# Square root on ScalarE, a six-slot ring for residual tiles and stores one cycle late, in a transformer layer on one core

## The chip, the cores and the metric

The kernel runs on one core of one Trainium2 chip, as one program with one launch. The metric is device time in microseconds (us), the median of several executions of the same program. The kernel before takes 717.07 us (three executions, 716.6 to 718.04). A profile adds what each engine did; the time of an execution is some 2 us more than the span from its first to its last instruction (708.25 against 706.2 in one execution of the changed kernel).

## The reference

One transformer layer: attention over a sliding window of 256 with 32 heads of 32, and a two-matrix MLP with silu, both behind a layer norm and with a residual. Everything is bf16, S = 2048, D = 1024, F = 3584.

```python
def _layernorm(x, axis=-1, eps=1e-5):
    m = jnp.mean(x, axis=axis, keepdims=True)
    v = jnp.var(x, axis=axis, keepdims=True)
    return (x - m) / jnp.sqrt(v + eps)

def reference(A_x, A_wqkv, A_wo, B_x, B_w1, B_w2):
    def _A_ref(x, wqkv, wo):
        ...  # 32 heads, causal window of 256, softmax(q k^T / sqrt(32)) v
        return o.transpose(0, 2, 1, 3).reshape(B, S, D) @ wo
    def _B_ref(x, w1, w2):
        return silu(x @ w1) @ w2
    x = A_x
    h = x + _A_ref(_layernorm(x), A_wqkv, A_wo)
    h2 = h + _B_ref(_layernorm(h), B_w1, B_w2)
    return h2
```

## The kernel before

The sequence is cut into four blocks of 512 rows, each of four tiles of 128. The order of instructions is written by hand (a manual schedule); nearly every transfer is issued by SyncE (SP), in program order. SP also waits: a transfer that isn't ready holds up every transfer behind it. A plan of the program, with the part names used below:

1. First block: statistics, reciprocal root and normalisation of the four tiles of x, transposes on TensorE, and the V projection, tile by tile; then Q and K of block 0.
2. Three loops of 24 cycles: attention of block b-1 beside V, Q and K of block b.
3. The last attention loop: 24 cycles of attention of block 3 beside the output projection of blocks 0 to 2, and beside the second layer norm of block 0, in single steps.
4. MLP of block 0. Its first h1 groups carry the end of the attention of the last head group (g = 7), and its h1 groups 6 to 13 the output projection of block 3. Then the MLP of blocks 1 to 3.

The first block. The tile's reciprocal root is an integer guess and three Newton steps, twelve small operations on VectorE, and one PSUM tile takes all eight transposes:

```python
def ln_rstd(st, rs, lo, hi):
    ...
    nc.vector.tensor_scalar(out=va, in0=st[:, lo:hi, 1], scalar1=LN_EPS, scalar2=None, op0=ALU.add)
    ...  # shift, subtract from 0x5F3759DF
    for _ in range(3):
        nc.vector.scalar_tensor_tensor(out=ta, in0=y, scalar=-0.5, in1=va, op0=ALU.mult, op1=ALU.mult)
        nc.vector.tensor_tensor(out=ta, in0=ta, in1=y, op=ALU.mult)
        nc.vector.scalar_tensor_tensor(out=y, in0=ta, scalar=1.5, in1=y, op0=ALU.add, op1=ALU.mult)

for j in range(4):
    ln_stats(x_ring[j], st, j)
    ln_rstd(st, rs, j, j + 1)
    ln_norm(x_ring[j], st, rs, j)
    ln_transpose(x_ring[j], lnT_b[0], j, act)
    v_group(0, j, 0, act)
    v_group(0, j, 1, act)
```

An output-projection group: eight matmuls, one for each head group's transposed attention output, then the residual add and, after the second half, the store of h. Two slots for the residual tile, two for the result:

```python
def load_res(b, j, src):
    nc.sync.dma_start(out=t_in[j % 2], in_=src[(b * 4 + j) * P:(b * 4 + j + 1) * P, :])

def wo_group(b, j, c):
    acc = next_acc()
    for g in range(G):
        nc.tensor.matmul(acc, lhsT=qT[b][:, g, j * P:(j + 1) * P], rhs=wo[:, g, c * 512:(c + 1) * 512], ...)
    nc.vector.tensor_tensor(out=t_out[j % 2][:, c * 512:(c + 1) * 512], in0=acc,
                            in1=t_in[j % 2][:, c * 512:(c + 1) * 512], op=ALU.add)
    if c == 1:
        nc.sync.dma_start(out=h_dram[...], in_=t_out[j % 2])
```

The last attention loop, and the start of the MLP:

```python
for g in range(G):
    for kind in KINDS:
        scores(NB - 1, g, kind)
        b, j, c = dense[n]
        if c == 0:
            ...
            load_res(nb, nj, x2d)          # the next tile's residual
        wo_group(b, j, c)
        if pending:
            pending.pop(0)()               # attention output of head group g-1; its end issues
                                           # the transpose of that group into qT
        ...                                # w1 rows, one every second cycle
        if n == 9:
            steps = ln2_steps(0)
            steps.pop(0)()                 # load of h, 1 MB, into h_blk
        if n == 17:
            nc.sync.dma_start(out=w2[0], in_=w2_v[:, 0:4, :])
        for _ in range(2 if n % 3 == 0 else 1):
            if steps and n >= 14:
                steps.pop(0)()             # 4 x statistics, rstd, 4 x norm, 4 x transpose
        n += 1
    pending = tail_of(NB - 1, g)
...
load_res(NB - 1, 0, x2d)
load_w2(5)
for b in range(NB):
    extra = []
    if b == 0:
        extra = [(f, 1) for f in pending]  # three parts: the last attention outputs and their transpose
    for ft in range(FT):
        acc = h1_group(b, ft)
        if extra:
            extra.pop(0)[0]()
            if not extra and b == 0:
                for i in (1, 2, 3, 4):
                    load_w2(i)             # 1 MB each
        silu(b, acc, ft)
        if b == 0 and 6 <= ft < 14:
            ...
            wo_group(NB - 1, j, c)
```

The softmax here doesn't subtract the row's maximum and nothing guards it: scores larger than these inputs give would overflow.

## Time and profile before

| | before |
|---|---|
| time, median (lowest, highest) | 717.07 us (716.6, 718.04) |
| span of the profiled execution (its time) | 717.0 us (718.72) |
| TensorE busy | 691.0 us |
| mean granted TensorE clock | 0.992 |

First from the page: the busy time of each engine, with its share of the span and its number of instructions. Then the view of waits, for TensorE (PE): which group of instructions stood idle, for whom, how long in all, how often, and the longest.

```profile
PE 691.0 (96%) x4916; PEld 333.4 (47%) x5006; DVE 292.9 (41%) x645; ACT 257.1 (36%) x325; POOL 172.8 (24%) x375
```

```profile
engine line waited for: us in total, times, longest us
PE acc L417 <- DMA r_a<-r_a: 6.6, 1, 6.6
PE acc L198 <- ACT r_w L179: 4.5, 4, 1.1
PE acc L216 <- DVE r_t L218: 3.8, 3, 1.6
```

L417 are the h1 matmuls, released by a transpose of the second norm; L198 are the V matmuls of the first block, which wait for ScalarE's copies of the transposes; L216 are the output-projection groups, which wait for an accumulator that VectorE's residual add (L218) frees. Together they are 15 us. Most of what else the change could give back is TensorE's slow clock around those holes: in the first block sixteen V matmuls take 5.20 us at a granted clock of 0.52 (9.5 to 13.0 us), and 3.63 later.

### The profile page before, as it was taken

Reading aid. Unit: us, or ns where it says so; the run is one execution under the profiler, and the core shown is the slowest. Engines: PE = TensorE matmul, PEld = TensorE weight load, DVE = VectorE, ACT = ScalarE, POOL = GpSimd, SP = SyncE. Lnnn points to the kernel's source line nnn. Section 1 sums busy time; section 2 is a strip of 40 time slices with the busy share of each in tenths; the row PEclk is TensorE's granted clock in tenths of the full one; section 3 lists DMA queues with packets and bytes.
Section 4 is the critical chain, followed back from the end, with each engine's and each line's share of the span. In section 5 each row is a group of like instructions: output and inputs, shape, how many; then the busy total and the mean of one; then the engine's idle time right before and its main releaser. Section 6 shows DMA issues by size and latency. Waiting matters only on the chain.

```text
span 717.0 us, 12077 instructions
## 1 busy us (share of the span) xinstructions
PE 691.0 (96%) x4916; PEld 333.4 (47%) x5006; DVE 292.9 (41%) x645; ACT 257.1 (36%) x325; POOL 172.8 (24%) x375
## 2 busy tenths in 40 slices
PE   7899999999999999869999999999999999999998
PEld 2444555555555555434444444444444444444443
DVE  7265745844344345724341613425133352234111
ACT  2315667777777776611230003310033200133000
POOL 1004657777777676600000000000000000000000
PEclk9999999999999999989999999999999999999999
DMA  9440133122401589757104140021310032300110
GB/s 312 157 91 28 23 61 89 24 46 52 135 17 23 134 278 326 217 146 296 45 2 138 60 111 0 1 65 54 81 37 0 1 96 61 80 1 0 30 37 22
DMA packets 75112, 60.56 MB, mean 84 GB/s; under 512 B 48944, under 2 KB 59184, under 8 KB 75056
## 3 DMA queue, kind: packets, MB, share of 16 engines
q1 hardware_dynamic: 75056, 59.78, 29.4%
q8 instruction: 39, 0.64, 0.4%
q14 instruction: 17, 0.14, 0.1%
HBM read 39.85 MB, written 8.39 MB: 67 GB/s over the span
## 4 chain that ended last, share of the span: by engine, by line
PE 91%; DMA 3%; DVE 2%; SPq 1%; ACT 1%; issue 1%; POOL 1%; DVEq 0%; POOLq 0%; ACTq 0%
PE hacc L417 18%; PE hacc L455 17%; PE acc L206 16%; PE acc L455 10%; PE acc L417 9%; PE acc L198 8%; PE o_ps L270 4%; PE sc L234 4%; PE acc L216 3%; DMA r_t<-in_A_x_dram 3%; PE hacc L216 1%; SPq L175 1%; DVE r_t L218 1%; POOL r_e L260 1%; ACT r_w L179 1%
## 5 line engine op out<-in xcount | busy, mean ns | idle before, releaser
L260 POOL TENSOR_SCALAR_AFFINE_SELECT r_e<-r_e 128x256 bf16<-128x256 bf16 (+1 forms) x368 | 169.9, 490 | 130.9 <-ACT r_e L245 127.4
L245 ACT ACTIVATE r_e<-sc 128x1024 bf16<-128x1024 f32 (+2 forms) x192 | 175.8, 967 | 70.2 <-PE sc L234 57.3
L417 PEld LDWEIGHTS <-r_w 128*128 128x128 bf16 x896 | 87.7, 98 | 112.4 <-issue 8.3
L455 PEld LDWEIGHTS <-r_a 128*128 128x128 bf16 x896 | 87.7, 98 | 105.7
L455 PE MATMUL hacc<-r_a 128*128 128x512 bf16 x548 | 121.7, 379 | 0.6
L417 PE MATMUL hacc<-r_e,r_w 128*128 128x512 bf16 x444 | 100.2, 379 | 0.6
L426 ACT ACTIVATE r_n<-hacc 128x512 f32<-128x512 f32 x30 | 17.9, 597 | 178.9 <-PE hacc L417 178.9
L455 PE MATMUL acc<-r_a 128*128 128x512 bf16 x328 | 73.6, 379 | 0.4
L206 PEld LDWEIGHTS <-r_w 128*128 128x128 bf16 x512 | 46.2, 98 | 58.6 <-issue 8.9
L208 DVE CAST r_a<-acc 128x512 bf16<-128x512 f32 x56 | 38.6, 690 | 84.6 <-PE acc L206 59.4
L270 PEld LDWEIGHTS <-r_e 128*128 128x128 bf16 x1440 | 50.4, 96 | 23.0 <-issue 0.6
L206 PE MATMUL acc<-r_t,r_w 128*128 128x512 bf16 x240 | 60.0, 380 | 0.8
L206 PE MATMUL acc<-r_w 128*128 128x512 bf16 x246 | 57.7, 380 | 0.5
L216 PE MATMUL acc<-r_o,r_a 128*128 128x512 bf16 x196 | 48.7, 380 | 4.5 <-DVE r_t L218 3.8
L270 PE MATMUL o_ps<-r_a,r_e 128*128 128x33 bf16 x1440 | 51.2, 178 | 0.0
L417 PE MATMUL acc<-r_e,r_w 128*128 128x512 bf16 x216 | 49.1, 379 | 0.0
L216 PEld LDWEIGHTS <-r_a 128*128 128x128 bf16 x256 | 23.4, 98 | 33.4 <-issue 8.8
L234 PE MATMUL sc<-r_a 32*128 32x128 bf16 (+2 forms) x704 | 37.2, 276 | 0.1
L468 DVE SCALAR_TENSOR_TENSOR r_t<-hacc,r_t 128x512 bf16<-128x512 f32 x20 | 13.6, 682 | 56.6 <-PE hacc L455 56.6
L198 PE MATMUL acc<-r_w 128*128 128x512 bf16 x122 | 31.0, 395 | 4.9 <-ACT r_w L179 4.5
L468 DVE SCALAR_TENSOR_TENSOR r_t<-acc,r_t 128x512 bf16<-128x512 f32 x12 | 8.3, 691 | 64.2 <-PE acc L455 59.7
L427 DVE SCALAR_TENSOR_TENSOR r_a<-r_n,hacc 128x512 bf16<-128x512 f32 x30 | 20.6, 688 | 33.0 <-ACT r_n L426 33.0
(58 smaller groups left out, 429.6 us busy)
## 6 DMA issues: line engine op xcount, KB each, us to landing
r_w<-in_B_w_dram SPq DMA_DIRECT2D x8, 896.0 KB, 6.6
r_a<-in_B_w_dram SPq DMA_DIRECT2D x7, 1024.0 KB, 5.6
r_w<-in_A_wqkv_dram SPq DMA_DIRECT2D x6, 1024.0 KB, 11.4
r_o<-in_A_x_dram SPq DMA_DIRECT2D x16, 256.0 KB, 5.1
r_t<-in_A_x_dram SPq DMA_DIRECT2D x16, 256.0 KB, 4.9
h_dram<-r_t SPq DMA_DIRECT2D x16, 256.0 KB, 4.0
r_t<-h_dram SPq DMA_DIRECT2D x16, 256.0 KB, 2.8
out_dram<-r_t SPq DMA_DIRECT2D x32, 128.0 KB, 1.7
```

The costliest lines, as they stand in the source:

```text
L198: nc.tensor.matmul(acc, lhsT=lnT_b[b % 2][:, kt, j * P:(j + 1) * P], rhs=wqkv[:, kt, col0:col0 + 512], start=(kt == 0), stop=(kt == KT - 1))
L206: nc.tensor.matmul(acc, lhsT=wqkv[:, kt, col0:col0 + P], rhs=lnT_b[b % 2][:, kt, :], start=(kt == 0), stop=(kt == KT - 1))
L208: copy(out=(qT, kT)[which][b][:, g, :], in_=acc)
L216: nc.tensor.matmul(acc, lhsT=qT[b][:, g, j * P:(j + 1) * P], rhs=wo[:, g, c * 512:(c + 1) * 512], start=(g == 0), stop=(g == G - 1))
L234: nc.tensor.matmul(sc[hh // 2][:, hh % 2, ch * P:(ch + nq) * P], lhsT=kT[t // 4][r0:r0 + DH, g, (t % 4) * P:(t % 4 + 1) * P], rhs=qT[b][r0 ...
L245: nc.scalar.activation(out=e[:, :, lo:hi], in_=sc[pair][:, :, lo:hi], func=ACT.Exp, scale=scale)
L260: nc.gpsimd.affine_select(out=ap, in_=ap, pattern=[[0, 2], [0, n], [sgn, P]], compare_op=ALU.is_ge if upper else ALU.is_gt, fill=0.0, base ...
L270: nc.tensor.matmul(o_ps[pair][:, qt * 2 + hh, 0:VW], lhsT=e_of(i, kind, pair)[:, hh, ch * P:(ch + 1) * P], rhs=v[:, b * 4 + kt, g * 4 + pa ...
L417: nc.tensor.matmul(acc, lhsT=w1[:, kt, ft * P:(ft + 1) * P], rhs=ln2T[b][:, kt, :], start=(kt == 0), stop=(kt == KT - 1))
L427: nc.vector.scalar_tensor_tensor(out=gT[:, ft, :], in0=th, scalar=1.0, in1=acc, op0=ALU.add, op1=ALU.mult)
L455: nc.tensor.matmul(acc, lhsT=gT[:, ft, j * P:(j + 1) * P], rhs=w2[ft // 4][:, ft % 4, c * 512:(c + 1) * 512], start=(ft == 0), stop=(ft == ...
L468: nc.vector.scalar_tensor_tensor(out=t_out[j % 2][:, c * 512:(c + 1) * 512], in0=acc, scalar=0.5, in1=t_in[j % 2][:, c * 512:(c + 1) * 512 ...
```

## The change

The intent is to remove these three. In the first block the root goes to ScalarE, the norm and the transposes are done in two halves (with two PSUM tiles), and tile j+1 is made ready before the V groups of tile j. The residual tiles of x get a ring of six slots, four of which lie in space of Q and K that is dead by then, so that they are loaded far ahead. The stores of h and the transposes of attention outputs go on a list `late` that is emptied at the start of the next cycle, so that SP doesn't wait for them while other transfers could be issued. The second norm's steps start two cycles earlier.

```diff
-    tp_ps = o_ps[1][:].rearrange("p a b -> p (a b)").bitcast(BF16)
+    tp_ps = [t[:].rearrange("p a b -> p (a b)").bitcast(BF16) for t in o_ps]
+    r_in = [view(r_a, 16384, 1024), view(r_a, 17408, 1024), *t_in, view(r_a, 22528, 1024), view(r_a, 23552, 1024)]
     load_x(0, 0)
-    load_wqkv(2 * D)
+    load_wqkv(2 * D, 0, 4)
     load_x(0, 1)
+    load_wqkv(2 * D, 4, 8)
     load_wqkv(2 * D + 512)
 ...
+    def ln_first(xt, st, rs, j):
+        ln_stats(xt, st, j)
+        nc.scalar.activation(out=rs[:, j:j + 1], in_=st[:, j, 1:2], func=ACT.Sqrt, bias=eps[:], scale=1.0)
+        nc.vector.reciprocal(out=rs[:, j:j + 1], in_=rs[:, j:j + 1])
+        for h in range(2):
+            ln_norm(xt[:, h * 512:(h + 1) * 512], st, rs, j)
+
+    def turn_first(xt, dst, j):
+        for h in range(2):
+            ...  # four transposes into tp_ps[h], then a ScalarE copy of 512 columns
 ...
+    def load_res(t):
+        nc.sync.dma_start(out=r_in[t % 6], in_=x2d[t * P:(t + 1) * P, :])
+    late = []
+    def run_late():
+        while late:
+            late.pop(0)()
 ...
-            nc.sync.dma_start(out=h_dram[...], in_=t_out[j % 2])
+            late.append(lambda: nc.sync.dma_start(out=h_dram[...], in_=t_out[j % 2]))
 ...
             attn_out(b, g, 11, 16)
-            attn_transpose(b, g)
+            late.append(lambda: attn_transpose(b, g))
 ...
+    ln_first(x_ring[0], st, rs, 0)
+    turn_first(x_ring[0], lnT_b[0], 0)
     for j in range(4):
-        ln_stats(...); ln_rstd(...); ln_norm(...); ln_transpose(...)
+        if j < 3:
+            ln_first(x_ring[j + 1], st, rs, j + 1)
         v_group(0, j, 0, act)
+        if j < 3:
+            turn_first(x_ring[j + 1], lnT_b[0], j + 1)
         v_group(0, j, 1, act)
+        if j == 2:
+            nc.scalar.activation(out=dummy[:], in_=eps[:], func=ACT.Exp)     # table load, early
 ...
-        return steps                                             # second norm: all norms, then all transposes
+        return steps[:-2] + [turns[0], steps[-2], turns[1], steps[-1]] + turns[2:]
 ...
     for g in range(G):                                           # last attention loop
         for kind in KINDS:
+            run_late()
+            if n % 2 == 0 and n >= 2 and n // 2 + 5 < S // P:
+                load_res(n // 2 + 5)
 ...
-            for _ in range(2 if n % 3 == 0 else 1):
-                if steps and n >= 14:
+            for _ in range(1 if n < 17 else 2):
+                if steps and n >= 12:
                     steps.pop(0)()
 ...
+    run_late()
     load_w2(5)
     ...
         for ft in range(FT):
             acc = h1_group(b, ft)
+            run_late()
             if extra:
                 extra.pop(0)[0]()
                 if not extra and b == 0:
                     for i in (1, 2, 3, 4):
                         load_w2(i)                               # unchanged
```

More of the change, by code (lines that the diff above doesn't have):

```diff
@@ L125, in load_x, with load_wqkv @@
         nc.sync.dma_start(out=x_ring[(b % 2) * 4 + j], in_=x2d[(b * 4 + j) * P:(b * 4 + j + 1) * P, :])
-    def load_wqkv(c0):
-        nc.sync.dma_start(out=wqkv[:, :, c0:c0 + 512], in_=wqkv_v[:, :, c0:c0 + 512])
+    def load_wqkv(c0, k0=0, k1=KT):
+        nc.sync.dma_start(out=wqkv[:, k0:k1, c0:c0 + 512], in_=wqkv_v[:, k0:k1, c0:c0 + 512])
     load_x(0, 0)
-    load_wqkv(2 * D)
+    load_wqkv(2 * D, 0, 4)
     load_x(0, 1)
+    load_wqkv(2 * D, 4, 8)
     load_wqkv(2 * D + 512)
@@ L140 @@
     make_identity(nc, ident[:])
+    eps = const.tile([P, 1], F32, name="eps")
+    nc.vector.memset(eps[:], LN_EPS)
     warm = ebuf[0]
@@ L171, in ln_norm, with ln_transpose @@
                                 op0=ALU.subtract, op1=ALU.mult)
-    def ln_transpose(xt, dst, j, copy):
-        if copy is None:
-            nc.sync.dma_start_transpose(out=dst[:, :, j * P:(j + 1) * P], in_=xt)
-            return
-        for kt in range(KT):
-            nc.tensor.transpose(out=tp_ps[:, kt * P:(kt + 1) * P], in_=xt[:, kt * P:(kt + 1) * P], identity=ident[:])
-        copy(out=dst[:, :, j * P:(j + 1) * P], in_=tp_ps.rearrange("p (k q) -> p k q", q=P))
+    def ln_transpose(xt, dst, j):
+        nc.sync.dma_start_transpose(out=dst[:, :, j * P:(j + 1) * P], in_=xt)
+    def ln_first(xt, st, rs, j):
[6 more added lines that the diff above has]
+        for h in range(2):
+            for i in range(4):
+                kt = h * 4 + i
+                nc.tensor.transpose(out=tp_ps[h][:, i * P:(i + 1) * P], in_=xt[:, kt * P:(kt + 1) * P], identity=ident[:])
+            nc.scalar.copy(out=dst[:, h * 4:(h + 1) * 4, j * P:(j + 1) * P],
+                           in_=tp_ps[h][:, 0:512].rearrange("p (k q) -> p k q", q=P))
     def ln_tiles(tag):
@@ L208, in qk_group, with load_h @@
         copy(out=(qT, kT)[which][b][:, g, :], in_=acc)
-    def load_res(b, j, src):
-        nc.sync.dma_start(out=t_in[j % 2], in_=src[(b * 4 + j) * P:(b * 4 + j + 1) * P, :])
+    def load_h(b, j):
+        nc.sync.dma_start(out=t_in[j % 2], in_=h_dram[(b * 4 + j) * P:(b * 4 + j + 1) * P, :])
+    def load_res(t):
[4 more added lines that the diff above has]
+            late.pop(0)()
     def wo_group(b, j, c):
@@ L218, in wo_group @@
         nc.vector.tensor_tensor(out=t_out[j % 2][:, c * 512:(c + 1) * 512], in0=acc,
-                                in1=t_in[j % 2][:, c * 512:(c + 1) * 512], op=ALU.add)
+                                in1=r_in[(b * 4 + j) % 6][:, c * 512:(c + 1) * 512], op=ALU.add)
         if c == 1:
-            nc.sync.dma_start(out=h_dram[(b * 4 + j) * P:(b * 4 + j + 1) * P, :], in_=t_out[j % 2])
+            late.append(lambda: nc.sync.dma_start(out=h_dram[(b * 4 + j) * P:(b * 4 + j + 1) * P, :], in_=t_out[j % 2]))
     def e_of(i, kind, pair):
@@ L302 @@
     st, rs = ln_tiles("a")
+    ln_first(x_ring[0], st, rs, 0)
+    turn_first(x_ring[0], lnT_b[0], 0)
     for j in range(4):
-        ln_stats(x_ring[j], st, j)
-        ln_rstd(st, rs, j, j + 1)
-        ln_norm(x_ring[j], st, rs, j)
-        ln_transpose(x_ring[j], lnT_b[0], j, act)
+        if j < 3:
+            ln_first(x_ring[j + 1], st, rs, j + 1)
         v_group(0, j, 0, act)
+        if j < 3:
+            turn_first(x_ring[j + 1], lnT_b[0], j + 1)
         v_group(0, j, 1, act)
+        if j == 2:
+            dummy = small.tile([P, 1], F32, name="dummy", tag="dummy")
+            nc.scalar.activation(out=dummy[:], in_=eps[:], func=ACT.Exp)
     for j in range(4):
@@ L319, in ln1_steps @@
             steps.append(lambda j=j: ln_norm(xs[j], st, rs, j))
-        return steps, [lambda j=j: ln_transpose(xs[j], lnT_b[b % 2], j, None) for j in range(4)]
+        return steps, [lambda j=j: ln_transpose(xs[j], lnT_b[b % 2], j) for j in range(4)]
     def ln2_steps(b):
@@ L330, in ln2_steps @@
             steps.append(lambda j=j: ln_norm(hb[:, j, :], st, rs, j))
-        for j in range(4):
-            steps.append(lambda j=j: ln_transpose(hb[:, j, :], ln2T[b], j, None))
-        return steps
+        turns = [lambda j=j: ln_transpose(hb[:, j, :], ln2T[b], j) for j in range(4)]
+        return steps[:-2] + [turns[0], steps[-2], turns[1], steps[-1]] + turns[2:]
     steps = sum(ln1_steps(1), [])
@@ L355 @@
             nc.sync.dma_start(out=wo[:, 4:8, :], in_=wo_v[:, 4:8, :])
+            load_res(0)
+            load_res(1)
         n = 0
@@ L376 @@
                 dense.append((b, j, c))
-    load_res(0, 0, x2d)
+    for t in range(2, 6):
+        load_res(t)
     steps = []
@@ L381 @@
         for kind in KINDS:
+            run_late()
+            if n % 2 == 0 and n >= 2 and n // 2 + 5 < S // P:
+                load_res(n // 2 + 5)
             scores(NB - 1, g, kind)
-            b, j, c = dense[n]
-            if c == 0:
-                nb, nj = (b, j + 1) if j < 3 else (b + 1, 0)
-                if nb < NB - 1:
-                    load_res(nb, nj, x2d)
-            wo_group(b, j, c)
+            wo_group(*dense[n])
             if pending:
@@ L427, in silu @@
         nc.vector.scalar_tensor_tensor(out=gT[:, ft, :], in0=th, scalar=1.0, in1=acc, op0=ALU.add, op1=ALU.mult)
-    load_res(NB - 1, 0, x2d)
+    run_late()
     load_w2(5)
@@ L437 @@
             acc = h1_group(b, ft)
+            run_late()
             if extra:
@@ L445 @@
                 j, c = divmod(ft - 6, 2)
-                if c == 0 and j < 3:
-                    load_res(NB - 1, j + 1, x2d)
                 wo_group(NB - 1, j, c)
-        load_res(b, 0, h_dram)
+        load_h(b, 0)
         if b == 0:
@@ L459 @@
             if j < 3:
-                load_res(b, j + 1, h_dram)
+                load_h(b, j + 1)
             accs = [next_acc(), next_acc()]
```

## The prediction

> **What bounds the kernel now.** I read the page first. TensorE is busy for 691.0 of 717.0 us and is 91% of the chain that ended last, so only TensorE's holes and its slow clock can be saved: 26 us at most, plus what the clock loses. The slices show where.
>
> ```profile
> PE   7899999999999999869999999999999999999998
> PEclk9999999999999999989999999999999999999999
> ```
>
> There are two weak places: the first two slices of 17.9 us, and the 18th and 19th (305 to 340 us). The waits of the whole run agree: between 60 and 236 us and after 320 us none is put down to PE. Then I read the timeline of 0 to 60 us:
>
> ```profile
> start us, us, engine line op out<-in xcount [idle before <-releaser]
> 1.52 5.51 PE L147 MATMUL sc<-r_e 128*128 128x512 bf16 x14 [1.52 <-DVE r_e L142]
> ...
> 4.96 0.21 DVE L154 BATCH_NORM_AGGREGATE st_a<-ln_st 128x2 f32<-128x12 f32 x1
> ...
> 7.52 0.55 DVE L170 TENSOR_SCALAR r_o<-r_o,st_a,rs_a 128x1024 bf16<-128x1024 bf16 x1
> ...
> 8.12 0.62 PE L178 MATMUL o_ps<-ident,r_o 128*128 128x128 bf16 x8 [1.09 <-DVE r_o L170]
> ...
> 8.78 1.01 ACT L179 COPY r_w<-o_ps 128x1024 bf16<-128x1024 bf16 x1 [6.69 <-PE o_ps L178]
> ...
> 9.84 5.20 PE L198 MATMUL acc<-r_w 128*128 128x512 bf16 x16 [1.10 <-ACT r_w L179]
> ...
> 27.07 3.63 PE L198 MATMUL acc<-r_w 128*128 128x512 bf16 x15 [1.15 <-ACT r_w L179]
> ...
> 30.54 27.79 PE L206 MATMUL acc<-r_w 128*128 128x512 bf16 x126
> ```
>
> Statistics end at 5.17, Newton's steps for the reciprocal root take VectorE to 7.48. Every tile then repeats transposes, a copy with TensorE idle 1.1 us, and 16 V matmuls. V takes 5.20 us the first time, 3.63 the last. Q/K begin at 30.54.
>
> Last, TensorE's timeline and the DMA queue's timeline at the end of attention:
>
> ```profile
> 244.24 1.89 PE L216 MATMUL acc<-r_o,r_a 128*128 128x512 bf16 x7 [0.87 <-DVE r_t L218]
> ...
> 276.37 1.89 PE L216 MATMUL acc<-r_o,r_a 128*128 128x512 bf16 x7 [1.39 <-DVE r_t L218]
> ...
> 293.48 1.89 PE L216 MATMUL acc<-r_o,r_a 128*128 128x512 bf16 x7 [1.57 <-DVE r_t L218]
> ...
> 302.88 0.53 PE L270 MATMUL o_ps<-r_a,r_e 128*128 128x33 bf16 x15
> 309.97 0.58 PE L417 MATMUL acc<-r_a,r_w 128*128 128x512 bf16 x1 [6.56 <-DMA r_a<-r_a]
> 310.77 2.76 PE L417 MATMUL acc<-r_a,r_w 128*128 128x512 bf16 x6 [0.22 <-DMA r_t<-in_A_x_dram]
> 313.33 0.57 PE L270 MATMUL o_ps<-r_a,r_e 128*128 128x33 bf16 x15
> ```
>
> ```profile
> 318.98 1.19 SPq L290 DMA_TRANSPOSE r_a<-r_n  x1
> 320.21 2.59 SPq L408 DMA_DIRECT2D r_a<-in_B_w_dram  x4
> 322.85 0.54 SPq L211 DMA_DIRECT2D r_t<-in_A_x_dram  x1
> ```
>
> Three output-projection groups wait for the residual add, which itself waits for residual loads. Then the first h1 group waits 6.56 us for transposes of the second layer norm, issued until 306.75, and starts slow.
>
> **What the Trainium skill says.** "TensorE: Matmul & The Clock Gate", Part 1: without recent work the array runs at half clock; the state is decided in free-running windows of about 3.4 us. The trace agrees: the V weight loads from 9.84 come every 0.43 us, from 13.15 twice as fast; the warm-up's last ones, near 6.2, were fast already, and the hole up to 9.84 cost that. "ScalarE: Activation LUTs", What ACT_TABLE_LOAD costs: 1283 ns a load, and square root and exp lie in different sets. The trace has one load of 1.28 us; the changed program has two. "DMA: Bandwidth & Descriptors", Queues, rings and completion order: within one issuer's ring the descriptors are taken in order. The trace agrees: the transpose issued at 270.50, alone 2.4 us, took 8.7 us and landed at 279.2, after a w1 load of 268.42 (9.7 us, 278.1); the residual load of 322.85, behind four w2 loads of 1 MB, took 11.7 us. So what stands behind megabytes in the SP order pays for them.
>
> **Part 1, the first block.** Statistics end at 5.2; square root on ScalarE (estimate 0.3 with a pointer bias, from the same skill section), reciprocal 0.2 (the attention reciprocals take 0.20), half a normalisation 0.3 (half of 0.55): ready at 6.1. But the 14 warm-up matmuls hold TensorE to 7.03, and some 0.15 more, since a memset of eps now precedes theirs. So transposes begin at 7.2 rather than 8.12, and the half copy (0.59 for 512 columns, as the V copies) releases V at 8.25 rather than 9.84. V of tile 0, half 0, needs both halves of the first weight megabyte; it landed at 6.6 before, about 8.0 now because x tile 1 goes between. From there transposes stand one tile ahead, so copies are hidden. Warm, V half 0 ends near 10.0, but weights of half 1 land only at 11.3 (issued 2.34, 9.0 to landing): start 11.3. Cold, it ends at 11.7, with transposes 12.2. Seven V groups of 1.73 and two more tiles of transposes at 0.5 follow: 13.1. VectorE and ScalarE just keep up: after a V group copy 0.59, root 0.3, reciprocal 0.2, half norm 0.3, against 1.73. The exp table load hides behind V of tile 3. Q/K begin at 24.4 to 25.5, not 30.54: gain 5.0 to 6.1, taken as 5.6. Q/K weights landed at 15.8 and 18.7, no bound.
>
> **Part 2, residual ring.** Tiles are loaded up to five ahead, the first two before the loop. The three waits go: 0.87 + 1.39 + 1.57 = 3.8 us. The rest of the loop, 24 cycles of about 2.57 us, is TensorE work and stays.
>
> **Part 3, second layer norm.** Its steps start two cycles earlier and go twice per cycle from cycle 17; transposes are issued after cycles 18 to 20, not 21 to 23. From cycle 20 to the loop's end are 4 x 2.57 = 10 us; two transposes of 1.3 us issue and 3.3 to landing fit. The h1 group starts where the loop ends. Before, from 303.41 to the next attention matmuls at 313.33 passed 9.9 us for 1.73 of work: gain 8.2, of which 6.8 is waiting and 1.4 the slow clock.
>
> **Part 4, what the lateness costs.** The last head group's transpose is now issued one h1 group later than its attention ends, but the four w2 loads stay where they were: in the changed order five w2 loads stand ahead of it, in the old only one. Call T0 the start of h1. The first four loads wait for nothing after T0+2; the fifth waits for the last attention matmuls, T0+6.6. Landings: the first 5.1 us after issue (as at 309.89), T0+7.1; then 2.7 us each (320.2 to 322.0 landed at 325.8, 328.5, 331.2, 333.9): the fifth T0+17.9, and the transpose behind it T0+18.6. The first output-projection group of the last block needs it in its eighth matmul. Before, it began 11.2 us after the second h1 group (313.76 to 324.95); adding 2.2 for the first gives T0+13.35, and seven matmuls of 0.216 make T0+14.9. New wait 3.8 us, and most likely a cold clock after it, 1.5 us, as after the old hole: loss 5.3.
>
> Sum: 5.6 + 3.8 + 8.2 - 5.3 = 12.3; less 0.3 for small waits of VectorE in the loop: 717.07 - 12.0 = 705.0 us, 1.7% less.
>
> **Rivals.** A: the late transpose is not held up. For it: it is small. Against: the order on the queue and the 8.7 us at 270.50. Then 699.7 us, faster by over 2%. B: VectorE becomes the bound in cycles 12 to 17. Per cycle it does an add 0.69 and a third of two norms of 0.62, 1.1 us; statistics add 1.5, the rstd chain 2.3 once. That is 2.6 against 2.57, and the block of h (1 MB, 8.4 us to landing at 266.49) must land by cycle 13. For it: that loop moves 257 GB/s. Against: two accumulators give one cycle of slack, and the load issues about 1 us earlier. It would cost 2 to 4 us: 707 to 709. C: in the first block root, table load or the order of V copies stall the transposes: the gain halves, 708. D: stores a cycle late hold the two output slots. A store took up to 8.6 us, and the slot is wanted some 7 us after issue, with a cycle of slack: hardly any loss.
>
> **Range and chances.** The gains of parts 1 to 3 are certain to about 1.5 us together; part 4 may cost 1 to 8. So 705.0, eight times in ten between 700.5 and 709.5. The 2% line is at 703.0: it takes a wait in part 4 of under about 2 us. Faster 0.25, within 2% 0.73, slower 0.02.
>
> **What would show it.** Q/K's first matmul near 25 us; no wait of the output projection for adds between 233 and 294; h1 starting within 0.5 us of the last attention matmuls, at about 294; then one hole of about 4 us, some 15 us later, ahead of the eighth matmul of an output-projection group, released by the DMA r_a<-r_n, whose transpose took over 8 us to land. No such hole makes part 4 wrong and the time 700; holes in cycles 12 to 18 would bring in B.

## The result, and the profile after

| | before | after |
|---|---|---|
| time, median (lowest, highest) | 717.0 us (716.6, 718.04) | 708.5 us (708.25, 710.91) |
| executions | 4 | 4 |
| span of the profiled execution (its time) | 717.0 us (718.72) | 708.9 us (710.91) |
| mean granted TensorE clock | 0.992 | 0.995 |

The ratio is 0.9887 with a 95% interval of 0.9863 to 0.9911. The output is correct. The change is a gain of 1.1%, inside the predicted range and at its slow end. Both profiled executions lie above the medians of their kernels, by 1.7 and 2.4 us, so their spans may be compared with each other: 8.1 us less.

The two rows of 40 slices show at once that one weak place is left (the 18th slice, 301 to 319 us):

```profile
PE   8999999999999999979999999999999999999998
PEclk9999999999999999989999999999999999999999
```

The view of TensorE's waits, after. L239 is the output projection (L216 before), L241 its add, L212 the V matmuls, L446 the h1 matmuls:

```profile
PE hacc L239 <- DMA r_a<-r_n: 5.3, 1, 5.3
...
PE acc L212 <- DMA r_w<-in_A_wqkv_dram: 1.5, 2, 1.2
PE acc L239 <- DVE r_t L241: 1.3, 1, 1.3
...
PE acc L446 <- issue: 0.2, 1, 0.2
```

The 6.6 us ahead of h1 are now 0.2, the waits for copies are nearly gone, and one wait for an add is left of three. In their place stands one wait of 5.3 us for `r_a<-r_n`, the transpose of an attention output.

TensorE's timeline in the first block, after (start, duration, engine and line, operation, number of instructions, and in brackets the idle time ahead of it and who ended it):

```profile
8.16 1.04 PE L212 MATMUL acc<-r_w 128*128 128x512 bf16 x4 [0.45 <-ACT r_w L192]
...
12.46 3.61 PE L212 MATMUL acc<-r_w 128*128 128x512 bf16 x16 [1.24 <-DMA r_w<-in_A_wqkv_dram]
...
25.57 14.62 PE L220 MATMUL acc<-r_w 128*128 128x512 bf16 x67
```

V starts at 8.16, not 9.84. Two waits for weights follow, 0.27 us until 9.46 and 1.24 us until 12.46; from there 16 V matmuls take 3.6 us each time without a hole. Q and K begin at 25.57 instead of 30.54.

TensorE's timeline from the last attention cycles on, after:

```profile
283.15 1.89 PE L239 MATMUL acc<-r_o,r_a 128*128 128x512 bf16 x8 [1.33 <-DVE r_t L241]
...
295.93 1.89 PE L446 MATMUL acc<-r_a,r_w 128*128 128x512 bf16 x8 [0.24 <-issue]
...
309.22 1.67 PE L239 MATMUL hacc<-r_o,r_a 128*128 128x512 bf16 x7
316.20 0.61 PE L239 MATMUL hacc<-r_o,r_a 128*128 128x512 bf16 x1 [5.31 <-DMA r_a<-r_n]
316.60 3.62 PE L446 MATMUL hacc<-r_a,r_w 128*128 128x512 bf16 x8
```

The h1 group starts 0.24 us after the attention matmuls. Then the first output-projection group of the last block runs seven matmuls and stops before the eighth, which reads head group 7. The next eight h1 matmuls take 3.62 us where eight take 1.89 elsewhere: the hole left TensorE at half clock (granted 0.50 from 316.2 to 319.7).

The timeline of SP's queue says why the eighth matmul waits. Columns as above; the duration is how long SP spent on issuing, waits included:

```profile
297.98 5.44 SPq L437 DMA_DIRECT2D r_a<-in_B_w_dram  x5
303.51 5.97 SPq L313 DMA_TRANSPOSE r_a<-r_n  x1
```

Five loads of w2, 1 MB each, are issued ahead of the transpose. It takes 12.6 us from issue to landing; in the kernel before the same transpose, issued at 318.98 with nothing large in flight, landed in 2.4 us. The view of its tile (`--tile r_n`, cut to the moment of issue) gives the landing, first after, then before:

```profile
L313 SPq DMA_TRANSPOSE r_a<-r_n x1: 5974/5974/5974, 303.5 to 303.5; - x1
DMA to landing us min/median/max: 12.6/12.6/12.6
```

```profile
L290 SPq DMA_TRANSPOSE r_a<-r_n x1: 1190/1190/1190, 319.0 to 319.0; - x1
DMA to landing us min/median/max: 2.4/2.4/2.4
```

Where the 8.1 us are, by the starts of the same work in the two traces:

| stretch | before | after | gain |
|---|---|---|---|
| first Q/K matmul | 30.54 | 25.57 | 5.0 |
| length of the last attention loop | 65.58 | 62.82 | 2.8 |
| end of the loop to the next attention matmuls (one h1 group) | 9.92 | 1.97 | 7.9 |
| start of the last block's first output-projection group to the second h1 group behind it: wait, then slow clock | 5.18 | 12.86 | -7.7 |

Between these the two traces run in step; the sum is 8.0 us.

### The profile page after: what moved, and what is told of

It reads as the page before. It is cut to its first block, busy times and chain, and to the rows that moved or that the text cites. A ratio compares the mean times of both kernels' runs of the same rounds, so it can differ in the third digit from the quotient of the medians.

```text
span 708.9 us, 12138 instructions
## 1 busy us (share of the span) xinstructions
PE 695.2 (98%) x5006; PEld 332.8 (47%) x5006; DVE 288.0 (41%) x606; ACT 259.7 (37%) x335; POOL 172.9 (24%) x375
## 4 chain that ended last, share of the span: by engine, by line
PE 94%; DMA 4%; DVE 2%; SPq 0%; issue 0%
PE hacc L446 18%; PE hacc L483 17%; PE acc L220 16%; PE acc L483 10%; PE acc L446 9%; PE acc L212 8%; PE acc L239 5%; PE o_ps L293 5%; PE sc L257 4%; DMA r_a<-r_n 2%; DMA r_w<-in_A_wqkv_dram 1%; PE hacc L239 1%; DMA r_a<-in_A_x_dram 1%; DVE ln_st L157 0%; DVE r_t L241 0%
## 5 line engine op out<-in xcount | busy, mean ns | idle before, releaser
L283 POOL TENSOR_SCALAR_AFFINE_SELECT r_e<-r_e 128x256 bf16<-128x256 bf16 (+1 forms) x368 | 169.9, 490 | 123.1 <-ACT r_e L268 119.7
L446 PEld LDWEIGHTS <-r_w 128*128 128x128 bf16 x896 | 87.8, 98 | 106.1 <-issue 2.4
L446 PE MATMUL hacc<-r_e,r_w 128*128 128x512 bf16 x456 | 100.9, 379 | 0.0
L220 PE MATMUL acc<-r_w 128*128 128x512 bf16 x256 | 58.2, 380 | 0.0
L239 PE MATMUL acc<-r_o,r_a 128*128 128x512 bf16 x208 | 49.4, 380 | 1.3 <-DVE r_t L241 1.3
L446 PE MATMUL acc<-r_e,r_w 128*128 128x512 bf16 x216 | 49.1, 379 | 0.0
L239 PEld LDWEIGHTS <-r_a 128*128 128x128 bf16 x256 | 23.3, 98 | 37.2 <-issue 7.4
L446 PE MATMUL hacc<-r_a,r_w 128*128 128x512 bf16 x144 | 34.6, 393 | 0.0
## 6 DMA issues: line engine op xcount, KB each, us to landing
r_w<-in_A_wqkv_dram SPq DMA_DIRECT2D x5, 1024.0 KB, 11.8
```

Of the source, the lines that this page charges most:

```text
L220: nc.tensor.matmul(acc, lhsT=wqkv[:, kt, col0:col0 + P], rhs=lnT_b[b % 2][:, kt, :], start=(kt == 0), stop=(kt == KT - 1))
L283: nc.gpsimd.affine_select(out=ap, in_=ap, pattern=[[0, 2], [0, n], [sgn, P]], compare_op=ALU.is_ge if upper else ALU.is_gt, fill=0.0, base ...
L446: nc.tensor.matmul(acc, lhsT=w1[:, kt, ft * P:(ft + 1) * P], rhs=ln2T[b][:, kt, :], start=(kt == 0), stop=(kt == KT - 1))
```

## The experiments

Theory: the three removals work as told, and a new loss of about 7.7 us stands against them, because the transpose of head group 7 lies behind megabytes of w2 on SP's queue. Rivals: that the lateness itself costs it (the transpose is issued one h1 group later); that the gains are smaller than they seem and the hole is only where a later bound shows; and that lateness is of no use, so that it could just be dropped. All twelve kernels gave a correct output, and each is told with the kernel before measured in the same rounds on the same chip (medians there 718.7 to 719.4 us).

### e1: the transpose ahead of the w2 loads

```diff
                 if not extra and b == 0:
+                    run_late()
                     for i in (1, 2, 3, 4):
                         load_w2(i)
```

> The changed kernel, with the last head group's transpose put ahead of the four w2 loads by running the late list before them. Theory (queue order): the 5.3 us wait ahead of the eighth matmul of the first late output-projection group and the slow clock after it go, together 7.7 us: 700.8 us, ratio to before about 0.977. Rival 1 (the transpose is slow for another reason, such as DMA traffic in general): it still takes over 8 us to land and the time stays near 708. Rival 2 (the wait only moves, to a w2 load or a residual): another hole of 3 to 5 us in the next 30 us, 704 to 706.

Measured: 700.52 us (700.13 to 702.5) against 718.7; ratio 0.9759 [0.9732, 0.9785]. SP's queue in this kernel:

```profile
300.58 1.19 SPq L313 DMA_TRANSPOSE r_a<-r_n  x1
301.83 2.50 SPq L437 DMA_DIRECT2D r_a<-in_B_w_dram  x4
```

The transpose lands 2.4 us after its issue, no wait of TensorE is left outside the first block, and the clock is 1.000. One line gives 8 us by the medians and 9 by the two ratios (0.9887 less 0.9759): the order on the queue is what the change lost. This kernel beats both.

### e2: the transpose still late, the loads later

```diff
                 extra.pop(0)[0]()
-                if not extra and b == 0:
-                    for i in (1, 2, 3, 4):
-                        load_w2(i)
 ...
             run_late()
+            if b == 0 and ft == 3:
+                for i in (1, 2, 3, 4):
+                    load_w2(i)
```

> The changed kernel, with the transpose as late as in the change (one h1 group later) but the four w2 loads moved behind it. If the order on the queue is the cause and the lateness of one h1 group (1.73 us) is harmless, it is as fast as the run with the transpose first: 700.8 us within 0.7. If the lateness itself costs the wait, the hole stays: 705 to 708.

Measured: 701.51 us (700.08 to 701.76), ratio 0.9760 [0.9731, 0.9790]. Here the transpose stands one h1 group late in the program, as in the changed kernel, and lands in 2.4 us. So that place costs nothing by itself; only what stands ahead of it on the queue does. Nor is it a delay in time, since SP runs ahead of TensorE and has nothing else to do: the transpose is issued 0.77 us after the last attention matmuls end, as in e1 (0.76); in the changed kernel it is 1.04. What is called late here is a place on the queue.

### e12: four loads ahead in place of five

```diff
                 if not extra and b == 0:
-                    for i in (1, 2, 3, 4):
+                    for i in (1, 2, 3):
                         load_w2(i)
 ...
             run_late()
+            if b == 0 and ft == 3:
+                load_w2(4)
```

> The changed kernel with one of the five w2 loads moved behind the late transpose, so four of 1 MB stand ahead. If the queue's megabytes are the cause, the transpose lands 2.7 us earlier: it takes about 10 us instead of 12.6, the wait shrinks from 5.3 to 2.6 us; the slow clock after it may go or stay (2.0 us): 703.7 to 705.7. If anything else holds it, the wait keeps its 5.3 us and the time 708.4.

Measured: 706.5 us (705.52 to 707.35), ratio 0.9816 [0.9787, 0.9844]. The eighth matmul's wait, in TensorE's timeline:

```profile
313.16 0.39 PE L239 MATMUL hacc<-r_o,r_a 128*128 128x512 bf16 x1 [2.96 <-DMA r_a<-r_n]
```

The landing took 10.6 us and the wait was 2.96 us, against 12.6 and 5.31 with one load more. A megabyte taken from the front is worth 2.0 us of landing and 2.35 us of waiting (the transpose was also issued 0.3 us sooner after the start of h1); between two landings in the changed kernel lie 2.7 to 2.9 us. The wait was expected at 2.6; the time came out 0.8 us above what was expected. The slow clock after the hole remained (the next eight h1 matmuls took 2.72 us), and this profile also has a wait of 1.5 us for an add, which is taken up below.

### e3: the kernel before, with four loads ahead of its transpose

```diff
             attn_out(b, g, 11, 16)
+            if (b, g) == (NB - 1, G - 1):
+                for i in (1, 2, 3, 4):
+                    load_w2(i)
             attn_transpose(b, g)
 ...
-                if not extra and b == 0:
-                    for i in (1, 2, 3, 4):
-                        load_w2(i)
```

> The kernel before, with the four w2 loads put between the last attention matmuls and their transpose, nothing late. If the queue order is the cause, the kernel before gets the hole of the changed one: a wait of 5 to 6 us for the transpose ahead of the first late output-projection group's last matmul, and a slow clock: 717 + 6 to 8 = 723 to 725. If the hole belongs to something else in the change (stores or residual ring), 717.

Measured: 720.75 us (718.48 to 721.59), ratio 1.0030 [1.0000, 1.0059]. The expectation of 723 to 725 missed. The transpose was indeed held up: issued at 318.44, it took 7.8 us and landed at 326.24. But its reader hardly waited:

```profile
324.46 2.19 PE L216 MATMUL hacc<-r_o,r_a 128*128 128x512 bf16 x8
```

A group of eight takes 1.89 us warm and here took 2.19. I had carried over the timing of the changed kernel and overlooked two differences: the loads began at 308.37, some 2 us earlier relative to the group, and the first h1 groups ran on the slow clock, so that the eighth matmul was due only at 325.97. The mechanism is there, the cost in this profile isn't: a late landing costs only what exceeds the reader's own lateness. That is also why it costs so much in the changed kernel, whose reader was brought forward. The profiled execution is the fastest of the four, though (718.48; the others took 720.24 to 721.59), and what the others waited for was not recorded; by its interval this order costs between nothing and 4.2 us.

### e4, e7, e8: one part of the change alone

e4 has the first block of the changed kernel and nothing else of it. e7 has the ring of residual tiles on the kernel before, with stores and transposes issued at once and the old steps of the second norm. e8 has only the earlier steps of the second norm. The core of e7 and e8:

```diff
 e7, on the kernel before
+    r_in = [...]                                   # six slots, as in the change
-                                in1=t_in[j % 2][:, c * 512:(c + 1) * 512], op=ALU.add)
+                                in1=r_in[(b * 4 + j) % 6][:, c * 512:(c + 1) * 512], op=ALU.add)
+            if n % 2 == 0 and n >= 2 and n // 2 + 5 < S // P:
+                load_res(n // 2 + 5)
 e8, on the kernel before
-        return steps
+        return steps[:-2] + [turns[0], steps[-2], turns[1], steps[-1]] + turns[2:]
-            for _ in range(2 if n % 3 == 0 else 1):
-                if steps and n >= 14:
+            for _ in range(1 if n < 17 else 2):
+                if steps and n >= 12:
```

> The kernel before with the first block of the change alone (root on ScalarE, half transposes a tile ahead, the split weight load). The trace of the changed kernel has Q/K begin 4.97 us earlier, and nothing until the last attention loop moves: 717.0 - 5.0 = 712.0. Rival: the earlier start is lost later in the DMA waits of the old residual scheme, whose waits would grow: 714 to 717.

> The kernel before with the residual ring alone (loads up to five tiles ahead, six slots), stores and transposes at once, old steps of the second norm. Theory: of the three waits for adds (0.87, 1.39, 1.57 us) the first two belong to residual loads and go; the third came with the norm's chain of small VectorE operations and stays. The wait of 6.6 us ahead of h1 stays and grows no more than 1 us: 2 to 3 us faster than before, ratio 0.996. Rival: the loads ahead unblock the queue and the norm's transposes too, so the 6.6 us shrink as well: ratio under 0.992.

> The kernel before with the second norm's earlier steps alone. Theory: the hole of 6.6 us ahead of h1 and its slow clock go nearly whole, but the statistics at cycle 12 now wait in VectorE's order for the load of h (landing near cycle 14), so adds behind them come late and the projection waits 2 to 4 us more: 4 to 6 us faster than before, ratio 0.992 to 0.994. Rival: the transposes still stand in the queue behind residual loads and stores and the hole stays above 4 us: ratio above 0.996.

| kernel | time, us (lowest, highest) | ratio [95%] | waits of TensorE that differ |
|---|---|---|---|
| e4, first block | 713.33 (712.91, 713.63) | 0.9931 [0.9907, 0.9955] | the 4.5 us for copies become 0.5; adds 3.8 to 4.9 |
| e7, ring | 715.35 (713.8, 716.09) | 0.9936 [0.9906, 0.9967] | adds 3.8 to 1.4; h1 6.6 to 5.9 |
| e8, norm steps | 713.17 (712.27, 715.26) | 0.9913 [0.9881, 0.9945] | h1 6.6 to 2.7; adds 3.8 to 6.1 |

e4 gives 4.95 us by its ratio, as its share in the accounting says; it came as expected. e7 kept the waits that were expected of it but gained 4.6 us by its ratio, not 2 to 3; e8 gained 6.3, not 4 to 6, although its hole shrank less than expected. e8 shows that the earlier norm steps alone buy the h1 hole partly with new waits for adds: VectorE stood still four times, 12.9 us in all, for residual loads (10.2 in the kernel before). In the changed kernel, with the ring, VectorE waits for no residual load; that the two parts need each other is not shown, as no run has just these two. e7 shows something that I had read wrongly in the profile before: with the residual tiles loaded far ahead, one of the three waits stays, 1.4 us. VectorE's timeline of the kernel before explains it (L161 begins the reciprocal root of the second norm, L167 ends it, L218 is the add):

```profile
289.68 0.17 DVE L161 TENSOR_SCALAR ln_var<-st_b 128x4 f32<-128x4 f32 x1
...
292.62 0.16 DVE L167 SCALAR_TENSOR_TENSOR rs_b<-ln_t,rs_b 128x4 f32<-128x4 f32 x1
292.74 0.69 DVE L218 TENSOR_TENSOR r_t<-acc,r_t 128x512 bf16<-128x512 f32 x1
```

The add that TensorE waited for at 293.48 stood behind three microseconds of the root's steps, not behind a load.

### e9: nothing late

e1 with the list taken away: stores of h and transposes are issued where they arise.

```diff
-            late.append(lambda: nc.sync.dma_start(out=h_dram[...], in_=t_out[j % 2]))
+            nc.sync.dma_start(out=h_dram[...], in_=t_out[j % 2])
 ...
-            late.append(lambda: attn_transpose(b, g))
+            attn_transpose(b, g)
```

> The run with the transpose first (e1), but stores and transposes issued at once as in the kernel before. Theory: with the ring in place the lateness is worth nothing, as the loads it lets by are needed only ten cycles later: 700.5 within 1.0. Rival: a store at the head of the queue holds up the load of h and the transposes of the norm, so that a hole of 1 to 3 us comes back ahead of h1 or in cycles 12 to 18: 702 to 704.

Measured: 708.54 us (706.79 to 708.87), ratio 0.9836 [0.9802, 0.9871]. The expectation missed, and the rival was right and more so. Two holes come back in TensorE's timeline, and behind each a group at half clock (3.57 and 3.39 us for eight matmuls):

```profile
282.92 3.57 PE L239 MATMUL acc<-r_o,r_a 128*128 128x512 bf16 x8 [1.73 <-DVE r_t L241]
...
299.78 3.39 PE L446 MATMUL acc<-r_a,r_w 128*128 128x512 bf16 x8 [2.64 <-DMA r_a<-r_a]
```

SP's queue shows the mechanism of the second one:

```profile
282.90 0.33 SPq L244 DMA_DIRECT2D h_dram<-r_t  x1
...
284.75 0.58 SPq L426 DMA_DIRECT2D r_a<-in_B_w_dram  x1
...
288.14 3.86 SPq L178 DMA_TRANSPOSE r_a<-r_a  x1
```

The load of w2[0] (L426) is now issued only after a store that SP had to wait for, at 284.75; in the changed kernel it goes out at 276.17, ahead of that wait. So its megabyte falls among the norm's transposes, the first of which need 7 to 8 us to land where 3.3 had been reckoned, and h1 waits for them. It looks like the mistake of the changed kernel in another place, but no run moves this load alone. The lateness, which I had treated as a cost alone, is worth 5.5 us by the two ratios (0.9836 less 0.9759, of 719) and 8.0 by the medians; that is for stores and transposes together, which no run separates, though the one that held w2[0] up was a store.

### e5, e6: the add that is still late

The changed kernel's one wait for an add, at 283.15, has two things ahead of it on VectorE. At 267.44 an add waited 2.89 us for a store to leave its slot (issued at 258.88, it took 8.5 us beside the 1 MB load of h), which put VectorE behind; and then came the reciprocal root of the second norm (L165 to L171), in VectorE's timeline after:

```profile
277.81 0.16 DVE L165 TENSOR_SCALAR ln_var<-st_b 128x4 f32<-128x4 f32 x1
278.00 0.63 DVE L166 TENSOR_SCALAR rs_b<-ln_var 128x4 int32<-128x4 int32 x1
...
279.99 0.16 DVE L171 SCALAR_TENSOR_TENSOR rs_b<-ln_t,rs_b 128x4 f32<-128x4 f32 x1
...
281.94 0.56 DVE L171 SCALAR_TENSOR_TENSOR rs_b<-ln_t,rs_b 128x4 f32<-128x4 f32 x1
282.42 0.68 DVE L241 TENSOR_TENSOR r_t<-acc,r_t 128x512 bf16<-128x512 f32 x1
```

Twelve operations took 4.7 us, single ones up to 0.63; in the first block of the kernel before the same twelve took 2.27 us, 0.16 each. GpSimd's timeline after, in the same stretch, shows when they are slow (L283 applies the attention mask):

```profile
277.97 1.98 POOL L283 TENSOR_SCALAR_AFFINE_SELECT r_e<-r_e 128x512 bf16<-128x512 bf16 x4 [0.89 <-ACT r_e L268]
280.50 1.98 POOL L283 TENSOR_SCALAR_AFFINE_SELECT r_e<-r_e 128x256 bf16<-128x256 bf16 x4 [0.55 <-ACT r_e L268]
```

The operations of 0.16 us lie ahead of the first burst of masks and in the pause from 279.95 to 280.50; those of 0.34 to 0.63 lie in the two bursts. The other profiles say the same: over all fourteen, the 76 operations of this chain that begin outside a burst take 0.16 or 0.17 us each, and of the 83 that begin inside one 74 take 0.27 to 0.66. The shape isn't it: a chain on 128x4 at 36.74 in the changed kernel, with GpSimd idle, takes 2.34 us.

e5 is e1 with a third slot for the result of the add; e6 is e1 with one Newton step in place of three in this one chain (the output stayed within tolerance).

```diff
 e5, on e1
+    r_x = big.tile([P, 1024], BF16, name="r_x")
+    h_out = t_out + [r_x[:, :]]
-        nc.vector.tensor_tensor(out=t_out[j % 2][...], ...)
+        nc.vector.tensor_tensor(out=h_out[(b * 4 + j) % 3][...], ...)
 e6, on e1
-        for _ in range(3):
+        for _ in range(rounds):                    # 1 for block 0 of the second norm, else 3
```

> The run with the transpose first (e1), with three output slots for h instead of two (2 KB more per partition). Theory: VectorE's wait for a landed store (2.9 us at cycle 12 of the changed kernel) goes, its small operations of the norm alone no longer use up the cycle of slack, and the wait of 1.3 us for adds, which some executions have and some have not, never shows: no wait for adds in the profile, 700.0, and a narrower spread than e1 (700.1 to 702.5). Rival: the wait comes from the norm's chain alone and stays: spread as in e1.

> The run with the transpose first (e1), with one Newton step instead of three in the second norm's first block (slightly less exact, still within the check). It takes six small VectorE operations, 1 to 3 us, out of cycle 16. If the chain is what makes adds late, no wait for adds: 700.0 and a narrow spread; if the store slots do, as e1.

Measured in five rounds: e5 701.19 us (700.3 to 701.56), ratio 0.9750 [0.9730, 0.9769]; e6 700.56 us (699.87 to 701.0), ratio 0.9742 [0.9723, 0.9761]. Neither profile has a wait for an add; in e5 VectorE's wait for the store is gone, in e6 it is still there (2.3 us). But the profile of e1, with neither, had no wait for an add either. So these runs tell nothing against the explanation and don't prove it: the wait of 0.4 to 1.7 us is there in the profiles of the changed kernel, e2, e9, e10 and e12, absent in e1, e5, e6 and e11, and in the time it is not seen. The profiles do show what it goes with. VectorE's wait for the store was 2.3 to 3.2 us in all of the changed kernel, e12, e10, e2, e1 and e6, and the chain took 4.7, 4.4, 4.6, 4.0, 3.6 and 1.7 us; TensorE then waited 1.3, 1.5, 1.3, 0.4, 0 and 0. So the wait goes with the length of the chain, and that with how it falls on GpSimd's bursts (e9, where the store held VectorE up otherwise, has 4.0 and 1.7).

### e10, e11: two further drafts

e10 is e1 with the V groups of the first block in another order (half 0 of tiles 0 and 1 first, and the second half of V's weights loaded behind x tile 2), to fill the wait for weights at 12.46. e11 has e10, e5's third slot and two Newton steps everywhere.

```diff
 e10, on e1
     load_wqkv(2 * D, 4, 8)
-    load_wqkv(2 * D + 512)
     load_x(0, 2)
+    load_wqkv(2 * D + 512)
 ...
+    v_group(0, 0, 0, act)
+    turn(1); prep(2)
+    v_group(0, 1, 0, act)
+    v_group(0, 0, 1, act)
```

> The run with the transpose first (e1), with x tile 2 loaded ahead of the second half of the V weights and V of tiles 0 and 1 done for half 0 before half 1. Theory: the missing 0.6 us of the first block were a wait for those weights (1.2 us in the changed kernel, landing near 12.4); with other work in that time Q/K begin 0.9 us earlier, near 24.6 us: 699.6. Rival: the transposes then wait for the layer norm instead and nothing is won: 700.5.

> All together: transpose first, three slots, two Newton steps everywhere, the other V order. If the parts are independent 699.0 to 699.5, faster than both kernels of the case; ratio to before 0.973 to 0.976.

Measured in the same five rounds as e5 and e6: e10 699.52 us (699.25 to 701.68), ratio 0.9735 [0.9716, 0.9755]; e11 700.08 us (699.54 to 700.2), ratio 0.9735 [0.9716, 0.9754]. From the first transposes to Q/K pass 17.15 us in e10 and 17.21 in e1: e1's wait for weights (0.7 us) is gone, and the waits for ScalarE's copies are 1.2 us instead of 0.5. Q/K begin at 23.78 in e10 and 24.61 in e1 mainly because the warm-up, which is the same in both, ended 0.8 us earlier. The 699.6 expected of e10 came true in the median, but not for the reason given; e11 missed its 699.0 to 699.5, and e5 and e6 came out above the 700.0 expected of them. Their intervals overlap with those of e1, e5 and e6, so none of the drafts can be called better than e1; e11 has the narrowest spread. All of them beat both kernels.

## Why the prediction was right, and where it was off

The time on record was 705.0 us and the measured one 708.5; the range held and the gain stayed under 2%, as was thought likeliest. The structure of the prediction held: three gains, and one new hole at the place that was named. No error cancelled another: all four parts came out worse than reckoned. Two slips in its sums change nothing: T0+18.6 less T0+14.9 is a wait of 3.7, not 3.8, and 2% below 717.07 is 702.7, not 703.0.

**Part 1, first block: predicted 5.6, traced 5.0, alone (e4) 4.95.** The steps came as told: V at 8.16 (8.25 predicted), V warm from there, the exp table load hidden (1.28 us, at 22.92, behind V; that square root and exp lie in different sets stands in the next section of the page named, Table sets: the hidden batching unit), Q/K at 25.57 (24.4 to 25.5). The small rest: weights of half 1 were awaited until 12.46 instead of 11.3. In the profile of e1, with the same first block, they were there by 11.50 and Q/K began at 24.61, so this rest differs from one execution to the next.

**Part 2, ring: predicted 3.8, traced 2.8.** The step that failed is "Three output-projection groups wait for the residual add, which itself waits for residual loads". It holds for two of three. The third wait of the kernel before (1.57 us) came from the reciprocal root on VectorE, as e7 shows, which keeps that wait; the changed kernel has 1.33 us of it, brought forward with the norm's steps. Rival B had the right engine and reckoned the chain at 2.3 us; it took 4.7.

**Part 3, second norm: predicted 8.2, traced 7.9.** Right. e8 and e9 add what the prediction didn't say: alone the earlier steps move the wait into the loop, and without the late stores 2.64 us of the hole come back.

**Part 4, the transpose behind w2: predicted -5.3, traced -7.7.** The mechanism was right in each of its links: e1 takes the order away and the loss is gone, e2 shows that lateness alone costs nothing, and e12 changes the load by one megabyte and the wait by 2.35 us. The term that was mis-sized is the landing. It was put at T0+18.6 and came at T0+20.2 (316.1, with T0 at 295.93): the first w2 load landed 5.7 us after its issue, not 5.1, the second 3.8 us later, not 2.7, and the other three after 2.7 to 2.9. The matmul that reads it was due where it was predicted, within 0.1 us. So the wait was 5.31 us in place of 3.8; the slow clock cost 2.0 in the next two groups in place of 1.5; a rest of 0.35 us lies in the group itself, whose eighth matmul also ran at half clock (0.40 us to the next start, not 0.22).

The differences are 0.6 + 1.0 + 0.3 + 2.4, less the 0.3 us that had been allowed for small waits of VectorE and are not seen: 12.0 predicted, 8.0 traced. Rival A, that the transpose isn't held up, was wrong for the change; its number, 699.7, is nearly what e1 measures with the transpose moved forward (700.52). Rival C didn't happen; its number, 708, and the range of rival B, 707 to 709, fit the measured 708.5 by chance. Rival D said "hardly any loss"; the slots did hold VectorE up for 2.89 us once, without a cost to TensorE that could be shown. What no rival named is the use of the lateness, 5.5 us by e9.

By the ratios of the parts, each times some 719 us (e4 4.95, e7 4.6, e8 6.3 us) the three together would be 15.8 us; e9, with all three and nothing late, has 11.8, and e1, with all three and the lateness, 17.3. The predicted gains of parts 1 to 3 were 17.6. Each of these ratios is known to about 2 us, so 15.8 and 11.8 are not clearly apart, while 11.8 and 17.3 are.

What stays open: by what means GpSimd's masks slow the small operations of VectorE (the profiles show that the two go together, but no run takes the masks away), whether the slow chain would make TensorE wait for an add without VectorE's wait for the store, and how much of e9's loss each kind of lateness saves.

## What to carry to other kernels

When a small transfer is put off by one step, look at which large ones pass it on the same queue: five megabytes ahead turned 2.4 us into 12.6, and one line of reordering was worth about as much as the whole change. A late landing costs only what exceeds the reader's own lateness, so a change that brings readers forward can expose a queue order that was harmless before (e3). And putting a store off is not just a cost, since a store that the issuing engine must wait for holds every load behind it (in e9 the load of w2[0] went out at 284.75 instead of 276.17).

## What the Trainium skill lacked or had wrong

- "TensorE: Matmul & The Clock Gate", HAM oscillation, warns of idle gaps over about 3.4 us. Shorter ones sufficed here: in e9 a gap of 1.73 us was followed by a group at half clock (eight matmuls in 3.57 us), and a gap of 2.64 us by another (3.39 us). In the changed kernel a gap of 1.33 us left the clock at 1.00. The page's next section tells of short idle times that cost the clock too, but gives no length. Why one short gap does and another doesn't, no run here shows.
- "DMA: Bandwidth & Descriptors", Queues, rings and completion order, gives the order and no figure for a small transfer behind large ones. The runs give one: the same transpose landed in 2.4 us alone, 10.6 us with four w2 loads of 1 MB issued ahead of it (e12), and 12.6 us with five (the changed kernel).
- "ScalarE: Activation LUTs", What ACT_TABLE_LOAD costs, counts some 2.66 us for a switch, a drain included. In the trace of the changed kernel the load itself took 1.28 us, as that section says, but it began 0.01 us after the activation ahead of it had ended (22.91), and the next activation began 1.29 us after the load's start: no drain was seen.
- "SBUF — State Buffer", SBUF: two separate sides, describes the port pair that VectorE and GpSimd share as an exclusive lock, without a figure for small operations. Twelve VectorE operations on 128x4 took 4.7 us beside GpSimd's masks and 2.34 us while GpSimd was idle: 0.16 or 0.17 us each outside the masks, mostly 0.27 to 0.66 among them; that the lock is the cause no run here shows.
